# Bias rows of a highway gate, in 64-column pieces among the shifted value matmuls of windowed attention

## Chip, cores and metric

One core of one Trainium2 chip. The metric is the device time of one execution in microseconds (us); the median of the runs is compared.

## What is computed

Attention with a sliding window of 128 keys and 4 sink keys (batch 4, 8 heads, 768 positions, 64 columns a head), then a highway layer on the 3072 tokens of 512 columns:

```
scores = q @ k.T / 8
keep   = key < 4  or  0 <= query - key < 128
a      = softmax(where(keep, scores, -1e9))
x      = a @ v                                  # heads side by side: 3072 x 512
H      = max(x @ w_h, 0)
T      = 1 / (1 + exp(-(x @ w_t + b_t)))
out    = T * H + (1 - T) * x
```

## The kernel before

The tokens are cut into 24 blocks of 128 queries (`n` = 0 to 23, six to a batch element). Everything of one block is done by named steps, and the string `ORDER` writes out by hand, as `step:block`, in which order the steps are issued. Each engine works through its own share of that list strictly in order; semaphores connect the engines. The schedule is software-pipelined: the scores of block n+1 stand ahead of the value product of block n, and the highway products of block n-1 behind it.

The steps that matter here, with the line that a profile shows for each:

- `Tq`, `Tk` or the first part of `S` (PE, L318): transposes of q and k; `tq`, `tk`, `tt` copy them to SBUF (ScalarE, L323 and L330; a `V` in the name puts the copy on VectorE).
- `S` (PE): scores. L371 are the 64 x 128 parts, L384 the 64 x 64 corner parts, in all four 64 x 64 quadrants of the array.
- `x0_`, `x1_`, `xx` (ScalarE, L393, L398): exponentials into `e`; `m0_`, `m1_`, `mm` (VectorE, L404): masks on them.
- `sk`, `es` (PE L353, ScalarE L360): scores of the sink keys and their exponentials.
- `A` (PE): the value product. L429 are sixteen shifted matmuls in two of the four quadrants (keys of the neighbouring blocks), L448 eight full ones, L454 two for the sinks. `A` also issues the loads for the block eight ahead on GpSimd's queue.
- `xh` (VectorE, L462 and L467): divides by the row sum, giving x.
- `X` (PE, L481): transposes x into spare columns of the same accumulator `av`; `xT` (ScalarE, L486) or `xTV` (VectorE, L486) copies that to SBUF.
- `Mh`, `Mt` (PE, L509 and L497): the two highway products; `u` (ScalarE, L502): tanh for the gate.
- `d`, `U`, `e`, `o` (VectorE, L515, L521, L526, L531): the blend; `o` also issues the store on SP.
- `wA` (PE, L646): warm-up matmuls on an unused accumulator.
- `Ta`, `Ha`, `Tb`, `Hb`, `ua`, `da`, and so on: the last block's highway layer in two halves.

Two facts set the order around the change. There is one `av` accumulator (`bufs=1`), so `A` of block n must come after the `xT` copy of block n-1. And there are two PSUM banks `m0` and `m1` for all of `sk`, `Mh` and `Mt`; the string `M_BANKS` says which of the two each request gets, in order. A request waits until the last reader of that bank is done: `es` for `sk`, `d` for `Mh`, `u` for `Mt`.

The bias of the gate is added on PE: a matrix with ones in one row, times `bt16`, which holds half the bias in rows 0 and 64. For blocks 8 to 22 this is done ahead of time, at the start of `A` of the next block, by two matmuls of 64 rows, 64 output partitions and 512 columns in the two quadrants on the diagonal (`pe_bias`, L437). For blocks 0 to 7 it is one full matmul at the start of `Mt` (L494).

Of the kernel before, what the change touches and what calls it, by code (L numbers as in the profile page):

```python
# [8 lines left out]
FP16 = mybir.dt.float16  # L9
# [11 lines left out]
def kernel(  # L21
# [18 lines left out]
    nc = tc.nc  # L40
    P = 128

    B, H, S, D = q.shape
# [17 lines left out]
    const = ctx.enter_context(tc.tile_pool(name="const", bufs=1))  # L61
# [24 lines left out]

    ctx.callback(close_s)
    HP = P // 2
    B0 = 9
    M0 = 9  # L90
    NV = AHEAD + 5
    NS4 = H * NSINK
# [43 lines left out]
    bt32 = const.tile([P, DM], FP32, tag="bt32")  # L136
    bt16 = const.tile([P, DM], FP16, tag="bt16")
    ones_row = const.tile([P, P], FP16, tag="ones_row")
    ones2 = const.tile([P, P], FP16, tag="ones2")
    kf_first = const.tile([P, H, D], FP32, tag="kf0", name="kf0")  # L140
    ident32 = const.tile([P, P], FP32, tag="ident32")
    ident2 = const.tile([P, P], FP16, tag="ident2")
# [45 lines left out]
    with tc.manual_schedule(engines={ENG.Pool, ENG.SP}):  # L188
# [7 lines left out]
        for b in range(B):  # L196
            nc.sync.dma_start(out=vs_dn[b], in_=v[b, :, 0:NSINK, :])
        nc.gpsimd.affine_select(
            out=ident, in_=ident, compare_op=ALU.is_equal, fill=0.0,
# [14 lines left out]
            out=bm, in_=bm, compare_op=ALU.is_ge, fill=0.0,  # L214
            base=0, pattern=[[-NSINK, H]], channel_multiplier=1)
        nc.gpsimd.affine_select(
            out=bm, in_=bm, compare_op=ALU.is_ge, fill=0.0,
# [39 lines left out]
    def bias_rows(_):  # L257
        nc.vector.memset(bt16, 0.0)
        nc.vector.memset(ones_row, 0.0)
        nc.vector.memset(ones_row[0:1, :], 1.0)  # L260
        nc.vector.tensor_copy(out=ones2, in_=ones_row)
        nc.vector.memset(ones2[HP:HP + 1, :], 1.0)

    def bias_half(_):
        for r in (0, HP):
# [2 lines left out]
    def sink_ones(_):  # L268
# [3 lines left out]

    m_bank = [m_ps.tile([P, DM], FP32, tag=f"m{i}", name=f"m{i}") for i in range(2)]
    M_BANKS = (
        "010101010101010101010101010010100101001100101011010110101101"
    )
    m_next = iter(M_BANKS)

    def m_tile():
        return m_bank[int(next(m_next))]  # L280
# [7 lines left out]
    av_t, xh_of, xT_of, t_of, u_of, h_of, dd_of, ee_of, sk_of = {}, {}, {}, {}, {}, {}, {}, {}, {}  # L288
# [124 lines left out]
    def e_at(n, h):  # L413
        return e_of[n][:, h // 4, h % 2, (h // 2) % 2, :]

    def av_tile(n):
        if n not in av_of:
            av_of[n] = av_ps.tile([P, 2, 4, P], FP32, tag="av", name="av")
            av_t[n] = av_of[n]
        return av_of[n]  # L420

    def pe_AB(n):
        av = av_tile(n)
        nxt = v_ring[(n + 1) % NV]
        prv = v_ring[(n - 1 if n % NSC else n) % NV]
        lo, hi = slice(0, HP), slice(HP, P)
        for j in range(H):
            for src, part, vt, h in ((lo, hi, nxt, j), (hi, lo, prv, (j + 4) % H)):
                nc.tensor.matmul(  # L429
                    av[part, h // 4, h % 4, 0:_AVN], lhsT=e_at(n, h)[src, P:EW],  # L430
                    rhs=vt[src, 65 * h:65 * h + _AVN], start=(h % 4 == 0), stop=False,
                    skip_group_check=True)

    def pe_bias(n):
        t_of[n] = m_tile()
        for rows in (slice(0, HP), slice(HP, P)):
            nc.tensor.matmul(t_of[n][rows, :], lhsT=ones2[rows, rows], rhs=bt16[rows, :],  # L437
                             start=True, stop=False, skip_group_check=True)

    def pe_A(n):  # L440
        if n >= B0:
            pe_bias(n - 1)
        pe_AB(n)
        av = av_of[n]
        vt = v_ring[n % NV]
        b, c = divmod(n, NSC)
        for h in range(H):
            nc.tensor.matmul(  # L448
                av[:, h // 4, h % 4, 0:_AVN], lhsT=e_at(n, h)[:, 0:P],
                rhs=vt[:, 65 * h:65 * h + _AVN], start=False,  # L450
                stop=False, skip_group_check=True)
        if c:
            for g in range(2):
                nc.tensor.matmul(  # L454
                    av[:, g, :, 0:65], lhsT=es_of[n],
                    rhs=vs_bd[b % 2][:, 4 * g:4 * g + 4, :], start=False, stop=True,
                    skip_group_check=True)
        av_of[n] = av.rearrange("p g h e -> p (g h) e")
# [178 lines left out]
    def do_A(n):  # L637
        pe_A(n)
        load_set(n + AHEAD)
# [5 lines left out]
    def spare(t):  # L645
# [12 lines left out]
        "Mh": pe_Mh, "Mt": pe_Mt, "u": act_u, "U": dve_U, "d": dve_d, "e": dve_e, "o": dve_o,  # L658
        "mz0_": first_mask, "mz1_": second_mask, "id": identities, "ma": clear_ks,
        "na": clear_vs, "mc": bias_rows, "fa": lambda _: fill_ks(0, nc.vector), "fb": bias_half,  # L660
        "fc": sink_ones, "fd": lambda _: sink_v(0, nc.vector), "cv": convert_v,
        "wA": lambda n: spare(av_tile(n)[:, 0].rearrange("p a b -> p (a b)")),
# [8 lines left out]
    }  # L671
    ORDER = """
    mz0_:0 ma:0 na:0 Tq:0 na:1 Tk:0 tq:0 mz1_:0 tk:0 ma:1 wA:0 wA:0 Tk:1 mc:0 cv:0 tk:1 fa:0
    wA:0 wA:0 wA:0 S:0 cv:1 x0_:0 fb:0 x1_:0 wA:0 wA:0 wA:0 wA:0 Tq:3 m0_:0 fc:0 tq:3 wA:0 Tk:2
    tk:2 m1_:0 fd:0 wA:0 wA:0 wA:0 wA:0 Tq:1 A:0 tq:1 S:1 xh:0 sk:1 x0_:1 x1_:1 Tq:2 m0_:1 X:0
    sk:3 xTV:0 es:1 Tk:3 m1_:1 tq:2 tk:3 wA:1 A:1 es:3 S:2 xh:1 x0_:2 x1_:2 Tk:4 m0_:2 sk:2
    tkV:4 X:1 es:2 m1_:2 S:3 xT:1 A:2 x0_:3 Mh:1 x1_:3 xh:2 tq:4 d:1 X:2 tk:5 Mh:0 xTV:2 m0_:3
    Mh:2 d:0 m1_:3 S:4 d:2 Mt:0 x0_:4 x1_:4 m0_:4 A:3 u:0 m1_:4 Mt:1 tq:5 xh:3 tk:6 U:0 sk:4 u:1
    e:0 S:5 es:4 o:0 X:3 x0_:5 U:1 sk:5 xTV:3 e:1 A:4 x1_:5 m0_:5 o:1 tq:6 Mt:2 xh:4 tk:7 es:5
    u:2 m1_:5 X:4 S:6 xT:4 U:2 e:2 A:5 x0_:6 o:2 Mh:3 x1_:6 xh:5 tq:7 Mh:4 m0_:6 tk:8 m1_:6 X:5  # L680
    d:3 S:7 xT:5 d:4 A:6 x0_:7 Mh:5 xh:6 x1_:7 Mt:3 d:5 tq:8 tk:9 m0_:7 X:6 u:3 m1_:7 Mt:5 xT:6
    U:3 e:3 sk:7 o:3 u:5 Tq:9 es:7 U:5 Mt:4 tq:9 e:5 o:5 S:8 u:4 U:4 A:7 x0_:8 e:4 o:4 Mt:6
    x1_:8 xh:7 tq:10 Mh:6 m0_:8 tk:10 m1_:8 u:6 X:7 d:6 S:9 xT:7 U:6 A:8 e:6 xx:9 o:6 sk:9 xh:8
    Mh:7 es:9 tt:9 mm:9 Mt:7 d:7 X:8 u:7 S:10 xTV:8 U:7 A:9 e:7 xx:10 o:7 Mt:8 xh:9 tt:10 Mh:8
    mm:10 u:8 X:9 d:8 S:11 xT:9 U:8 A:10 e:8 xx:11 o:8 sk:11 xh:10 Mt:9 es:11 tt:11 mm:11 Mh:9
    u:9 X:10 d:9 S:12 xT:10 U:9 A:11 e:9 xx:12 o:9 Mt:10 xh:11 tt:12 Mh:10 mm:12 u:10 X:11 d:10
    S:13 xT:11 U:10 A:12 e:10 xx:13 o:10 sk:13 xh:12 Mt:11 es:13 tt:13 mm:13 Mh:11 u:11 X:12
    d:11 S:14 xT:12 U:11 A:13 e:11 xx:14 o:11 Mh:12 xh:13 tt:14 Mt:12 mm:14 X:13 d:12 u:12 S:15
    xT:13 U:12 e:12 xx:15 A:14 o:12 sk:15 xh:14 Mt:13 tt:15 mm:15 es:15 X:14 S:16 u:13 xTV:14
    U:13 A:15 xx:16 Mh:14 xh:15 tt:16 Mt:14 d:14 mm:16 Mh:13 u:14 U:14 sk:17 d:13 X:15 es:17  # L690
    S:17 xT:15 e:13 e:14 A:16 xx:17 o:13 o:14 Mt:15 xh:16 tt:17 Mh:15 mm:17 u:15 X:16 S:18 d:15
    xT:16 U:15 A:17 xx:18 e:15 o:15 Mh:16 xh:17 tt:18 Mt:16 mm:18 X:17 u:16 S:19 xTV:17 d:16
    A:18 xx:19 U:16 e:16 sk:19 xh:18 Mt:17 es:19 mm:19 tt:19 Mh:17 o:16 u:17 X:18 S:20 d:17
    xT:18 U:17 A:19 xx:20 e:17 o:17 Mh:18 xh:19 tt:20 Mt:18 mm:20 X:19 u:18 S:21 xTV:19 d:18
    A:20 xx:21 U:18 e:18 sk:21 o:18 Mt:19 es:21 xh:20 tt:21 Mh:19 mm:21 u:19 X:20 S:22 d:19
    xT:20 U:19 A:21 xx:22 e:19 o:19 Mh:20 xh:21 tk:24 Mt:20 mm:22 X:21 u:20 S:23 xTV:21 d:20
    A:22 xx:23 U:20 e:20 sk:23 xh:22 Mt:21 es:23 mm:23 X:22 u:21 Mh:21 xT:22 o:20 A:23 d:21 U:21
    Mt:22 xh:23 e:21 X:23 u:22 Mh:22 xTV:23 o:21 Ta:23 d:22 Ha:23 ua:23 U:22 e:22 Tb:23 da:23
    o:22 Hb:23 ub:23 db:23 ea:23 eb:23 pa:23 pb:23
    """  # L700

    with tc.manual_schedule(engines={ENG.PE, ENG.DVE, ENG.Activation, ENG.SP, ENG.Pool}):
        warm_up(8)
        identities(0)
        for step in ORDER.split():
            op, n = step.split(":")
# [36 lines left out]
```

## Time and profile before

| | us |
|---|---|
| Median of 3 runs | 122.24 |
| Lowest, highest | 121.48, 125.95 |
| The profiled execution: device time | 121.67 |
| The profiled execution: first to last instruction (span) | 119.5 |
| PE busy | 107.5 |
| VectorE (DVE) busy | 105.0 |
| ScalarE (ACT) busy | 87.8 |
| GpSimd (POOL) busy | 72.6 |
| Old bias pairs (L437), 30 matmuls | 5.9 |
| Full bias matmuls (L494), 8 matmuls | 3.0 |

Times within the profile count from its first instruction. PE matmuls are pipelined and overlap in the records: one 512-column matmul is shown with 0.38 us, while four in a row start 0.22 us apart. So starts are compared, not lengths. In the timeline a row gives the start, the length up to the end of the last instruction of the group, the engine, the line, the operation, the tiles and shapes, the number of instructions, and in brackets the idle time of the engine before it with what ended it.

### The profile page before, as it was taken

To read this page: it belongs to the slowest core of one execution; us is meant where nothing else is said; L and a number is where in the kernel's file an instruction comes from. 1 tells how busy PE (TensorE), PEld (TensorE's weight loads), DVE (VectorE), ACT (ScalarE), POOL (GpSimd) and SP (SyncE) were. 2 spreads that over 40 slices of the span, in tenths; PEclk is the share of its full clock that TensorE was granted. 3 is DMA by queue.
4 is the path that set the end of the run, shared out by engine and by line. 5 is a ranking of instruction groups with operands and counts; after the bars stand their busy time and mean duration, and the time that the engine had idled before them with its cause. 6 is when DMAs were issued, how large, how long until landed. Compare 5 with 4: busy or idle time off the path is not lost.

```text
span 119.5 us, 4971 instructions
## 1 busy us (share of the span) xinstructions
PE 107.5 (90%) x2119; PEld 65.5 (55%) x2119; DVE 105.0 (88%) x252; ACT 87.8 (73%) x123; POOL 72.6 (61%) x97
## 2 busy tenths in 40 slices
PE   5998676999899999799998999999999999999920
PEld 1443454655765546556754665657556665565610
DVE  6889666596999899999999999969999999999990
ACT  2248196929998978788898999987998979773210
POOL 5999886959799799967779999986000000000000
PEclk9999999999999999999999999999999999999995
DMA  2999999999999999999999999999920222011132
GB/s 55 217 172 153 146 180 174 194 153 151 128 194 209 207 137 183 191 205 205 177 195 219 118 198 157 205 203 157 207 84 12 89 92 93 26 67 73 52 139 88
DMA packets 79848, 17.64 MB, mean 148 GB/s; under 512 B 75602, under 2 KB 76882, under 8 KB 79828
## 3 DMA queue, kind: packets, MB, share of 16 engines
q0 software_dynamic: 71888, 9.97, 134.2%
q1 hardware_dynamic: 6884, 7.12, 19.2%
q10 hardware_dynamic: 1056, 0.26, 1.3%
q8 instruction: 16, 0.26, 0.9%
q14 instruction: 4, 0.03, 0.1%
HBM read 21.01 MB, written 6.29 MB: 228 GB/s over the span
## 4 chain that ended last, share of the span: by engine, by line
PE 63%; DVE 16%; DMA 7%; ACT 4%; issue 3%; POOL 3%; DVEq 0%; ACTq 0%
PE m L509 15%; PE m L497 11%; DMA qsd<-in_q_dram 7%; PE av L448 6%; PE av L429 6%; PE sps L384 4%; PE sps L318 4%; PE sps L371 4%; PE av L481 4%; DVE xh L467 4%; DVE otok L531 3%; PE av L454 3%; ACT e L393 3%; PE m L353 2%; DVE e L404 2%
## 5 line engine op out<-in xcount | busy, mean ns | idle before, releaser
L404 DVE TENSOR_TENSOR e<-e,mask 128x768 f16<-128x768 f16 (+1 forms) x33 | 24.8, 758 | 2.4 <-ACT e L393 2.3
L398 ACT ACTIVATE e<-sps,ebias 128x1536 f16<-128x1536 f32 x15 | 23.1, 1542 | 3.2 <-PE sps L384 3.0
L121 POOL DMA_DIRECT2D v<-in_v_dram x26 | 22.2, 854 | 4.7 <-DVE t L323 1.0
L509 PE MATMUL m<-wh_sb,xT 128*128 128x512 f16 x92 | 23.5, 379 | 0.3 <-issue 0.3
L497 PE MATMUL m<-wt_sb,xT 128*128 128x512 f16 x92 | 23.6, 379 | 0.0
L114 POOL DMA_DIRECT2D ksd<-in_k_dram x26 | 22.3, 861 | 2.0 <-DMA v<-in_v_dram 1.8
L107 POOL DMA_DIRECT2D qsd<-in_q_dram x23 | 21.2, 924 | 1.0 <-DMA qsd<-in_q_dram 0.5
L393 ACT ACTIVATE e<-sps,ebias 128x768 f16<-128x768 f32 x18 | 15.3, 898 | 5.3 <-PE sps L384 4.8
L502 ACT ACTIVATE u<-m 128x512 f16<-128x512 f32 x23 | 13.7, 597 | 6.5 <-PE m L497 6.3
L467 DVE TENSOR_TENSOR xh<-av,rec 128x512 f16<-128x512 f32 x24 | 16.6, 691 | 0.8
L531 DVE SCALAR_TENSOR_TENSOR otok<-xh,ee 128x512 f32<-128x512 f16 x23 | 15.8, 688 | 0.6
L515 DVE SCALAR_TENSOR_TENSOR dd<-m,xh 128x512 f16<-128x512 f32 x23 | 15.7, 686 | 0.1
L509 PEld LDWEIGHTS <-xT 128*128 128x128 f16 x92 | 8.6, 98 | 9.1 <-issue 1.0
L497 PEld LDWEIGHTS <-xT 128*128 128x128 f16 x92 | 8.8, 98 | 8.0
L330 ACT COPY tt<-sps 128x1024 f16<-128x1024 f16 x13 | 13.0, 999 | 0.0
L323 ACT COPY t<-sps 128x512 f16<-128x512 f16 x19 | 10.4, 590 | 2.1 <-PE sps L318 2.1
L429 PEld LDWEIGHTS <-e 64*64 64x64 f16 x384 | 9.9, 107 | 2.7 <-issue 1.9
L429 PE MATMUL av<-v,e 64*64 64x66 f16 x384 | 10.8, 193 | 0.4 <-DVE xT L486 0.3
L448 PE MATMUL av<-v,e 128*128 128x66 f16 x192 | 10.4, 195 | 0.0
L526 DVE TENSOR_TENSOR ee<-u,dd 128x512 f16<-128x512 f16 x23 | 9.7, 427 | 0.7
L486 ACT COPY xT<-av 128x512 f16<-128x512 f16 x15 | 8.7, 581 | 1.7 <-PE av L481 1.6
L481 PEld LDWEIGHTS <-xh 64*128 64x128 f16 x192 | 4.2, 95 | 10.2 <-DVE xh L467 7.4
(94 smaller groups left out, 173.5 us busy)
## 6 DMA issues: line engine op xcount, KB each, us to landing
out_dram<-otok SPq DMA_DIRECT2D x23, 256.0 KB, 4.7
qsd<-in_q_dram POOLq DMA_DIRECT2D x23, 128.0 KB, 7.2
ksd<-in_k_dram POOLq DMA_DIRECT2D x19, 128.0 KB, 7.1
v<-in_v_dram POOLq DMA_DIRECT2D x19, 128.0 KB, 7.1
wh_sb<-in_moe_w_h_dram POOLq DMA_DIRECT2D x1, 512.0 KB, 7.9
wt_sb<-in_moe_w_t_dram POOLq DMA_DIRECT2D x1, 512.0 KB, 8.4
ksd<-in_k_dram POOLq DMA_DIRECT2D x7, 64.0 KB, 6.9
v<-in_v_dram POOLq DMA_DIRECT2D x7, 64.0 KB, 6.3
```

The lines of the kernel that those rows point to most:

```text
L107: nc.gpsimd.dma_start(out=qsd, in_=q[b, :, c * P:(c + 1) * P, :].transpose([1, 0, 2]))
L114: nc.gpsimd.dma_start(out=ksd[rows], in_=k[b, :, s0:s0 + nr, :].transpose([1, 0, 2]))
L121: nc.gpsimd.dma_start(out=vt[rows, :, 0:D], in_=v[b, :, s0:s0 + nr, :].transpose([1, 0, 2]))
L393: nc.scalar.activation(out=e_tile(n)[:, g].rearrange("p a b c -> p a (b c)"), in_=s_tile(n, g)[:, :, 0:2 * EW], func=AF.Exp, bias=ebias, s ...
L398: nc.scalar.activation(out=e_tile(n).rearrange("p g a b c -> p (g a) (b c)"), in_=s_of[n][:, :, 0:2 * EW], func=AF.Exp, bias=ebias, scale= ...
L404: nc.vector.tensor_tensor(out=ev, in0=ev, in1=m.unsqueeze(1).to_broadcast([P, k, EW]), op=ALU.mult)
L429: nc.tensor.matmul(av[part, h // 4, h % 4, 0:_AVN], lhsT=e_at(n, h)[src, P:EW], rhs=vt[src, 65 * h:65 * h + _AVN], start=(h % 4 == 0), sto ...
L448: nc.tensor.matmul(av[:, h // 4, h % 4, 0:_AVN], lhsT=e_at(n, h)[:, 0:P], rhs=vt[:, 65 * h:65 * h + _AVN], start=False, stop=False, skip_g ...
L467: nc.vector.tensor_tensor(out=xh.rearrange("p (h d) -> p h d", d=D), in0=av_of.pop(n)[:, :, 0:D], in1=rec_of.pop(n).unsqueeze(2).to_broadc ...
L497: nc.tensor.matmul(t_of[n], lhsT=xT[:, kc, :], rhs=wt_sb[:, kc, :], start=False, stop=(kc == NOC - 1), skip_group_check=True)
L509: nc.tensor.matmul(hps, lhsT=xT[:, kc, :], rhs=wh_sb[:, kc, :], start=(kc == 0), stop=(kc == NOC - 1))
L531: nc.vector.scalar_tensor_tensor(out=otok, in0=xh_of.pop(n), scalar=2.0, in1=ee_of.pop(n), op0=ALU.mult, op1=ALU.add)
```

## The change

The bias of the gate is no longer two matmuls of 512 columns ahead of the shifted value matmuls. It is sixteen matmuls of 64 columns: after each pair of shifted matmuls in `pe_AB` come two pieces, one in each of the diagonal quadrants. A table `T_BESIDE` says which block's bias is hosted by which `A`. From block 9 on these are the same blocks as before; the bias of blocks 1, 2, 3, 6 and 7, which was a full matmul in `Mt`, is now hosted too, by `A` of blocks 3, 4, 6, 7 and 8. Blocks 0, 4 and 5 keep the full matmul. `ones_row` now has its ones in two half rows, so that it serves both forms, and `ones2` is dropped.

`M_BANKS` and `ORDER` are written anew for it. PE's own order of steps is the same but for one `wA` more. On ScalarE and VectorE some steps change place or engine: `tq:3` and `xT:4` go to VectorE; `xT:19`, `xT:21` and `xT:23` go to ScalarE; `xTV:3` stands ahead of `U:1`; `o:1`, `o:2`, `e:16` and `o:20` are moved; `es:21` stands behind `tt:21`; at the end `e:21` stands ahead of `xh:23`.

```diff
-    B0 = 9
+    T_BESIDE = {3: 1, 4: 2, 6: 3, 7: 6, 8: 7, 9: 8, 10: 9, 11: 10, 12: 11, 13: 12, 14: 13, 15: 14, 16: 15, 17: 16, 18: 17, 19: 18, 20: 19, 21: 20, 22: 21, 23: 22}
...
-        nc.vector.memset(ones_row[0:1, :], 1.0)
-        nc.vector.tensor_copy(out=ones2, in_=ones_row)
-        nc.vector.memset(ones2[HP:HP + 1, :], 1.0)
+        nc.vector.memset(ones_row[0:1, 0:HP], 1.0)
+        nc.vector.memset(ones_row[HP:HP + 1, HP:P], 1.0)
...
-        "010101010101010101010101010010100101001100101011010110101101"
+        "010101010101010010101000101101011010110011010100101001010010"
...
+        m = T_BESIDE.get(n)
+        if m is not None:
+            t_of[m] = m_tile()
         for j in range(H):
             for src, part, vt, h in ((lo, hi, nxt, j), (hi, lo, prv, (j + 4) % H)):
                 nc.tensor.matmul(
                     av[part, h // 4, h % 4, 0:_AVN], lhsT=e_at(n, h)[src, P:EW],
                     rhs=vt[src, 65 * h:65 * h + _AVN], start=(h % 4 == 0), stop=False,
                     skip_group_check=True)
-
-    def pe_bias(n):
-        t_of[n] = m_tile()
-        for rows in (slice(0, HP), slice(HP, P)):
-            nc.tensor.matmul(t_of[n][rows, :], lhsT=ones2[rows, rows], rhs=bt16[rows, :],
-                             start=True, stop=False, skip_group_check=True)
+            if m is not None:
+                cols = slice(D * j, D * j + D)
+                for part in (lo, hi):
+                    nc.tensor.matmul(
+                        t_of[m][part, cols], lhsT=ones_row[part, part], rhs=bt16[part, cols],
+                        start=(j == 0), stop=False, skip_group_check=True)
 
     def pe_A(n):
-        if n >= B0:
-            pe_bias(n - 1)
         pe_AB(n)
...
-    A:18 xx:19 U:16 e:16 sk:19 xh:18 Mt:17 es:19 mm:19 tt:19 Mh:17 o:16 u:17 X:18 S:20 d:17
-    xT:18 U:17 A:19 xx:20 e:17 o:17 Mh:18 xh:19 tt:20 Mt:18 mm:20 X:19 u:18 S:21 xTV:19 d:18
-    A:20 xx:21 U:18 e:18 sk:21 o:18 Mt:19 es:21 xh:20 tt:21 Mh:19 mm:21 u:19 X:20 S:22 d:19
-    xT:20 U:19 A:21 xx:22 e:19 o:19 Mh:20 xh:21 tk:24 Mt:20 mm:22 X:21 u:20 S:23 xTV:21 d:20
-    A:22 xx:23 U:20 e:20 sk:23 xh:22 Mt:21 es:23 mm:23 X:22 u:21 Mh:21 xT:22 o:20 A:23 d:21 U:21
-    Mt:22 xh:23 e:21 X:23 u:22 Mh:22 xTV:23 o:21 Ta:23 d:22 Ha:23 ua:23 U:22 e:22 Tb:23 da:23
-    o:22 Hb:23 ub:23 db:23 ea:23 eb:23 pa:23 pb:23
...
+    d:16 A:18 xx:19 U:16 sk:19 xh:18 Mt:17 es:19 mm:19 tt:19 Mh:17 e:16 u:17 X:18 o:16 S:20
+    xT:18 d:17 A:19 xx:20 U:17 e:17 Mh:18 o:17 tt:20 xh:19 Mt:18 mm:20 X:19 u:18 S:21 xT:19 d:18
+    xx:21 A:20 U:18 e:18 o:18 sk:21 Mt:19 tt:21 xh:20 es:21 mm:21 u:19 Mh:19 U:19 X:20 d:19 S:22
+    xT:20 e:19 xx:22 A:21 o:19 Mh:20 xh:21 tk:24 Mt:20 mm:22 X:21 d:20 u:20 S:23 xT:21 U:20 e:20
+    xx:23 A:22 o:20 sk:23 xh:22 Mt:21 es:23 mm:23 X:22 u:21 Mh:21 xT:22 U:21 A:23 d:21 e:21
+    Mt:22 xh:23 o:21 u:22 X:23 Mh:22 xT:23 U:22 Ta:23 d:22 Ha:23 ua:23 e:22 Tb:23 da:23 o:22
+    Hb:23 ub:23 ea:23 db:23 eb:23 pa:23 pb:23
```

## The prediction

> **What bounds the kernel now.** I read the page first (busy shares, then the chain that ended last), then stretches of 8 us by engine, then the timeline around the calls that the change touches.
>
> ```profile
> PE 107.5 (90%) x2119; PEld 65.5 (55%) x2119; DVE 105.0 (88%) x252; ACT 87.8 (73%) x123; POOL 72.6 (61%) x97
> PE 63%; DVE 16%; DMA 7%; ACT 4%; issue 3%; POOL 3%; DVEq 0%; ACTq 0%
> ...
> 30.00:54.00 24.00, 22.80 (x479) 14.17 (x478) 22.90 (x46) 20.65 (x34) 21.77 (x27) 1.00 2.28 182
> 54.00:62.00 8.00, 8.00 (x189) 5.06 (x180) 7.79 (x16) 7.21 (x10) 5.85 (x9) 1.00 2.17 194
> ```
>
> The columns after the length are busy time of PE, PEld, DVE, ACT and POOL. Two engines are full at once. From 30 to 54 us the chain runs mostly through DVE; from 54 to 110 us mostly through PE, a block every 3.7 us (4.1 with a sink step), with DVE at 97%.
>
> The decisive view is what ends PE's wait before A of a block. Block 11, then 14:
>
> ```profile
> 61.30 0.29 PE L481 MATMUL av<-ident,xh 64*128 64x64 f16 x8
> 61.63 0.59 ACT L486 COPY xT<-av 128x512 f16<-128x512 f16 x1
> 61.98 0.32 PE L384 MATMUL sps<-tt 64*64 64x64 f16 x16
> 62.12 0.39 PE L437 MATMUL m<-bt,ones 64*64 64x512 f16 x2
> 62.27 0.45 PE L429 MATMUL av<-v,e 64*64 64x66 f16 x16
> ...
> 73.28 0.60 ACT L502 ACTIVATE u<-m 128x512 f16<-128x512 f32 x1 [0.28 <-PE m L497]
> 73.78 0.58 ACT L486 COPY xT<-av 128x512 f16<-128x512 f16 x1
> 73.94 0.39 PE L437 MATMUL m<-bt,ones 64*64 64x512 f16 x2
> 74.41 0.45 PE L429 MATMUL av<-v,e 64*64 64x66 f16 x16
> ```
>
> xT:n-1 reads the one av buffer that A:n overwrites. It ends at 61.63+0.59 = 62.22 and the shifted value matmuls (L429) start at 62.27; in block 14 at 74.36 and 74.41. In all fifteen blocks with a bias pair L429 starts 0.05 to 0.07 us behind the end of that copy. PE issues its last score matmul at about 61.98+0.32-0.20 = 62.10, so the pair at 62.12 only fills a wait of 0.17 us. The chain names L437 because the pair runs there, not because it decides.
>
> **What the skill says.** "TensorEngine Tiling (Array Packing)", Key Properties: tiles work independently, and a change of tiling mode drains the array. The trace agrees: L384 uses all four 64x64 quadrants, and its 16 matmuls start within 0.32-0.20 = 0.12 us, 0.03 us for each four; L429 uses two quadrants, and its 8 pairs start within 0.45-0.19 = 0.26 us, also 0.03 us a pair. The same page, Gotcha 1, warns of two row tiles in one PSUM bank; the old pair already writes one bank from both row halves, to different partitions. "PSUM — Partial Sum Buffer", The four PSUM rules: a starting matmul clears the written-bits of its whole bank in the quadrants that it writes, and a later one without start overwrites where the bit is clear. So start on piece 0 alone does what the change needs; no time follows from it.
>
> ```profile
> 108.89 0.40 PE L437 MATMUL m<-bt,ones 64*64 64x512 f16 x2
> 108.96 0.45 PE L429 MATMUL av<-v,e 64*64 64x66 f16 x16
> 109.34 0.33 PE L448 MATMUL av<-v,e 128*128 128x66 f16 x5
> ...
> 21.67 0.44 PE L429 MATMUL av<-v,e 64*64 64x66 f16 x16
> 22.05 0.43 PE L448 MATMUL av<-v,e 128*128 128x66 f16 x8
> ```
>
> Block 23 has the pair 0.07 us ahead of L429, so both run together; block 2 has none. L429 to L448 is 0.38 us in both: bias beside the shifted matmuls is already free.
>
> **The change part by part.**
>
> *1. The fifteen old pairs go (blocks 9 to 23).* Gain 0: the wait for xT stays and is now bare.
>
> *2. Sixteen pieces in each of 20 calls of A.* PE gets 20x16 = 320 matmuls and loses 30+5, and one warm-up is added. Not shown before: eight groups of four in a row, with a reload of the ones each time. Below: 0 (a gain is excluded, since xT sets the start). Above: the pieces take turns with the shifted pairs, 8x0.032 = 0.26 us a call. I take 0 by the L384 row, which has the same four quadrants and as many loads. The first piece is a new wait inside A: for the last reader of its bank. Behind it on PE stand the rest of A and all that follows. From block 9 that reader is u:n-2, as for the old pair, and it ends ahead of xT. For the early hosts it is d:2 (ends 26.79, A:3 starts 27.79), es:4 (30.78 against 31.83), d:3 (about 37.5 against 38.3), es:7 (43.98 against 45.57) and u:6 (48.88 against 50.12): cost 0.
>
> *3. Five full bias matmuls go (Mt of 1, 2, 3, 6, 7).* L494 to L497 is 0.22 us (52.31 to 52.52), together 1.1 us of PE. At 28 to 50 us DVE is the queue that is late, so I book nothing directly; Mt:7's counts in 5.
>
> *4. DVE from 28 to 50 us.* xTV:3 ahead of U:1 and the copy of xT:4 moved from ACT to DVE let A:4 start about 0.2 us and A:5 about 0.5 us earlier, but DVE gains one copy of 0.42 us. Its queue from the end of o:0 (31.16) to the end of d:4 (39.25) was full but for 0.13 us: 39.25+0.41-0.13 = 39.53. Mh:5 now takes the bank of d:4 (before, of d:3) and so starts at 39.58 instead of 39.43; Mh:5 takes 0.86+0.17 us to its end, d:5 waits for it, 40.66 instead of 40.49: **+0.17 us**, which the full DVE queue carries on to 54 us. POOL work here also stretches DVE (two L404 took 1.86 us at 41.10 against 0.55 each at rest, beside L181 on POOL): the shift may move that by ±0.8 us.
>
> *5. The new bank string.* Holding t7 from A:8 leaves one bank for sk:9 and Mh:7, so Mh:7 waits for es:9.
>
> ```profile
> 51.44 1.03 PE L509 MATMUL m<-wh_sb,xT 128*128 128x512 f16 x4
> 51.71 0.45 ACT L360 ACTIVATE es<-m,ebias 32x256 f16<-32x256 f32 x1
> ...
> 54.24 0.42 DVE L486 COPY xT<-av 128x512 f16<-128x512 f16 x1
> 54.71 0.45 PE L429 MATMUL av<-v,e 64*64 64x66 f16 x16
> ```
>
> Mh:7 moves from 51.44 to 51.71+0.45+0.05 = 52.21; minus the 0.22 us of Mt:7's bias, X:8 comes near 53.97 instead of 53.48. xTV:8 sits behind mm:9 and d:7 on DVE and ran at 54.24; with +0.17 on DVE it runs at 54.41, and X:8 is done by 54.26. A:9 starts 0.17 us late. From A:9 to A:19 queue orders on PE and ACT are unchanged: the offset stays, **sum so far +0.17**.
>
> *6. xT:19 and xT:21 go from DVE to ACT.*
>
> ```profile
> 97.04 0.60 ACT L502 ACTIVATE u<-m 128x512 f16<-128x512 f32 x1 [0.27 <-PE m L497]
> 97.40 0.42 DVE L486 COPY xT<-av 128x512 f16<-128x512 f16 x1
> 97.87 0.45 PE L429 MATMUL av<-v,e 64*64 64x66 f16 x16
> ...
> 99.43 0.45 ACT L360 ACTIVATE es<-m,ebias 32x256 f16<-32x256 f32 x1
> 100.06 1.03 PE L509 MATMUL m<-wh_sb,xT 128*128 128x512 f16 x4
> ```
>
> On ACT the copy queues behind u:18, as block 14 shows (u at 73.28, copy 0.50 us later). So 97.04+0.50+0.58+0.05 = 98.17 for A:20 against 97.87: **+0.29**. Then es:21 now stands behind tt:21. xx:21 begins at 98.0 as before, tt:21 at 99.45, es:21 0.89 us later at 100.34, ending at 100.79. Mh:19 has the bank of es:21: 100.84, where 100.06+0.29 = 100.35 was due: **+0.49**, less 0.1 us by which PE came late to X:20 before (101.02, where Mh:19's four would have let it start at 100.06+0.86 = 100.92). A:21 comes near 102.66 against 101.99 (+0.67). In block 22 u:20 began at 104.85: 104.85+0.67+0.50+0.58+0.05 = 106.65 against 105.61: **+1.04** in all for this part. A:23 is bound by xT:22 and keeps it. DVE, 0.42 us lighter in each of the two blocks, is no help: PE is what runs late there.
>
> *7. The tail.* xTV:23 (0.42 us at 111.36) leaves DVE, and e:21 stands ahead of xh:23. Da waits for PE's L569, so of 0.42 us about 0.41 is kept: **-0.42**. The rest (tq:3 on DVE and one copy of ones fewer before 13 us, one more warm-up, fb, fc) lies in front of A:0, which starts at 13.6 after a DMA wait with the mask 0.7 us ready: 0. The steps o:1, o:2, e:16 and o:20 are moved by under 2 us; each o also issues its block's store on SP, which has nothing else queued, and otok has four buffers: 0. The loads that each A issues on POOL keep their order; the ones of A:4 and A:5 go out a little earlier.
>
> Sum: +0.17+1.04-0.42 = **+0.8 us**. Against the profiled execution's 121.67 us (span 119.5 and 2.2 around it): 122.5. The median of the three runs is 122.24, the lowest 121.48; the profile lies in the lower half, so I say 122.7.
>
> **The rivals.**
> *A, slower: the pieces are not hidden.* Place: the L429 run of A:9 to A:23. Price: up to 0.26 us x 15 = 3.8, with the five early hosts behind DVE: 122.5+3.8 = 126.3. It decides once a group of four takes more than about 0.05 us instead of 0.03. For it: 64 instructions in 0.26 us is a longer burst than L384's, and three banks are written at once. Against: the L384 and block 23 rows. Chance 0.24.
> *B, a little faster: the stalls of 5 and 6 don't appear* because the queues shift by themselves, and the early starts of A:4 and A:5 are kept: 121.67-0.42-0.4 = 120.9. For it: A:5 really has 0.5 us; against: DVE has one copy more. Chance 0.13.
> *C, clearly faster: the pair was real PE time*, 0.14 us from L437 to L429: 15x0.14+5x0.22 = 3.2, 118.5. Against: L429 sits at the end of xT in fifteen of fifteen. Chance 0.07.
> The forecast has 0.56.
>
> **How the numbers follow.** The forecast's own range is 121.5 to 123.9: ±0.8 for POOL beside DVE, and PE issue gaps (0.31 and 0.79 us were seen at 64.6 and 18.95) with 13% more PE instructions. To hold 8 in 10 it reaches down to B and up to A: 120.9 to 126.3. Within 2% (119.8 to 124.7, about what a measurement of this kernel can tell from no change): B, the forecast but 0.05, and some of A. Faster by over 2% is C; slower is A and that 0.05.
>
> **What would show it.** Right: starts of L429's successor still 0.05 us behind an xT copy in every hosted block; first shifted matmul to L448's first still 0.38 us; A:20 and A:22 0.3 to 0.5 us further behind their score matmuls; Mh:7 and Mh:19 behind es; PE busy lower in 28 to 50 us without an earlier A:9. Wrong: 0.5 us or more in place of 0.38 (A); A starting right behind the scores (C); A:9 before 54.3 (B).

## The result, and the profile after

The changed kernel takes 130.7 us in the median (130.1 to 133.4) against 122.7: ratio 1.065, 95% interval 1.054 to 1.077. The forecast was 122.7 with a range up to 126.3. It is slower, and by far more than the steps of the sum or the slower rival allowed.

Executions of one kernel scatter by some per cent, the longer ones often at a lower mean clock of the array: the ratios leave the longer ones out, and since the profiled execution (133.37 us, span 131.7) is one of them, places and kinds of loss are read from it and amounts from the comparisons. From its page, the busy line, the clock row in 40 slices, the instruction queue and the chain by engine:

```profile
PE 110.9 (84%) x2405; PEld 67.2 (51%) x2405; DVE 104.3 (79%) x250; ACT 88.4 (67%) x124; POOL 72.2 (55%) x97
...
PEclk9999999999999999998569999559999999999997
...
q8 instruction: 19, 0.31, 0.9%
...
PE 48%; DVE 22%; issue 12%; ACT 6%; DMA 5%; POOL 3%; DVEq 0%; ACTq 0%
```

"issue", time in which the engine waited for nothing that the profile shows, went from 3% to 12% of the chain. DVE has no more work than before. The clock has two dents that were not there. The waits of PE on "issue" (total us, times, longest), both of the kernel before and then the four longest after:

```profile
PE sps L384 <- issue: 0.8, 1, 0.8
PE m L509 <- issue: 0.3, 1, 0.3
...
PE m L437 <- issue: 4.0, 2, 2.5
PE av L447 <- issue: 2.9, 1, 2.9
PE m L508 <- issue: 0.7, 1, 0.7
PE m L351 <- issue: 0.7, 1, 0.7
```

In the timeline the long ones after are single holes, in the midst of matmuls that wait for no one:

```profile
55.58 0.19 PE L437 MATMUL m<-bt,ones_row 64*64 64x64 f16 x1 [1.55 <-issue]
...
62.55 0.60 PE L447 MATMUL av<-v,e 128*128 128x66 f16 x8 [2.88 <-issue]
...
83.06 0.26 PE L437 MATMUL m<-bt,ones_row 64*64 64x64 f16 x1 [2.50 <-issue]
```

The key is where they stand. Count PE's records (weight loads, matmuls and its few semaphore instructions) in order of start. Every one of these holes stands at number 194 plus a multiple of 256: 962, 1218, 1986, 2242 and 3010 in this profile. In the kernel before, the two holes, 0.8 us at 19.7 us and 0.3 us at 64.9 us, stand at 450 and 2242: the same series. Call these numbers borders. And q8 is, by its counts, the queue of PE's own instructions: 16 packets for 4279 records before, 19 for 4852 now, one packet of 16 KB for each border. Its line before:

```profile
q8 instruction: 16, 0.26, 0.9%
```

So PE runs out of instructions. The trace has the start of each q8 packet. While the loads of q, k and v run (to 85 us) it begins 1.1 to 4.6 us after PE has passed the border before (3.0 in the mean), takes 0.9 to 1.5 us, and at every long hole PE resumes 1.3 to 1.8 us after it has landed. When the loads have ended the packets begin 0.6 us after the border in the mean (from 0.9 us ahead of it to 1.8 behind), and no hole is left. In the kernel before the packets are no earlier: 2.9 us behind the border in the mean while the loads run. What has changed is how soon PE needs them. The hole at 62.55: border passed at 55.58, packet from 60.11 to 61.07, resumed at 62.55.

In this execution the holes have a second price. The window of the hole, and that of the work behind it (busy PE, PEld, DVE, ACT, POOL, then the granted clock):

```profile
59.60:62.55 2.95, 0.07 (x9) 0.09 (x1) 0.94 (x2) 1.24 (x1) 1.98 (x4) 0.82 2.23 185
62.55:67.36 4.81, 4.81 (x22) 2.19 (x22) 1.76 (x3) 1.85 (x3) 4.69 (x7) 0.50 1.92 167
```

After 2.9 us without work the clock is 0.50 through the 4.8 us that follow. The same steps (A of block 10 from L447 on, sk, Mt, Mh) took 2.5 us in the kernel before: 2.3 us more, and by the same reckoning about as much again after 83.06. Holes (7.2 us more than before) and dents (4.6) together come to 11.8 of the 12.2 us by which this profile is longer. The other executions bear less of it: the one with a mean clock of 0.996 took 130.1 us, those with 0.973 and 0.974 took 129.7 to 130.8, so most of the loss is there without a dent.

The Trainium skill, "TensorE: Matmul & The Clock Gate", Part 1, has the array's clock halved after an idle window of some 3.4 us. Here shorter holes did it, though not always: in all the profiles, seven of the eight holes of over 2 us (2.1 to 3.0 from start to start) were followed by a dent of 3.4 or 6.8 us, and one of 2.7 us, in the changed kernel shifted by 112 records, was not.

What the forecast did see is there too:

```profile
117.62 0.22 PE L430 MATMUL av<-v,e 64*64 64x66 f16 x2 [0.53 <-ACT xT L485]
...
118.00 0.43 PE L447 MATMUL av<-v,e 128*128 128x66 f16 x8
```

From the first shifted matmul to the first full one it is 0.38 us, with sixteen pieces between as without; it is 0.36 to 0.38 us in 16 of the 20 hosted blocks; of the others, three have a hole between the two and one lies in a dent. And A waits for xT.

### The profile page after: what moved, and what is told of

It is laid out like the page before. It is cut to its first block, busy times and chain, and to the rows that moved or that the text cites. A ratio compares the mean times of both kernels' runs of the same rounds, so it can differ in the third digit from the quotient of the medians.

```text
span 131.7 us, 5545 instructions
## 1 busy us (share of the span) xinstructions
PE 110.9 (84%) x2405; PEld 67.2 (51%) x2405; DVE 104.3 (79%) x250; ACT 88.4 (67%) x124; POOL 72.2 (55%) x97
## 3 DMA queue, kind: packets, MB, share of 16 engines
q0 software_dynamic: 71888, 9.97, 124.4%
## 4 chain that ended last, share of the span: by engine, by line
PE 48%; DVE 22%; issue 12%; ACT 6%; DMA 5%; POOL 3%; DVEq 0%; ACTq 0%
PE m L508 11%; PE m L496 9%; DMA qsd<-in_q_dram 5%; PE av L447 5%; DVE xh L466 5%; DVE otok L530 5%; PE av L430 3%; PE sps L316 3%; DVE dd L514 3%; DVE e L402 3%; PE av L480 3%; PE sps L369 3%; PE m L351 3%; PE av L453 3%; PE sps L382 3%
## 5 line engine op out<-in xcount | busy, mean ns | idle before, releaser
L508 PE MATMUL m<-wh_sb,xT 128*128 128x512 f16 x92 | 24.4, 390 | 1.6 <-ACT es L358 0.9
L402 DVE TENSOR_TENSOR e<-e,mask 128x768 f16<-128x768 f16 (+1 forms) x33 | 23.8, 731 | 2.2 <-ACT e L391 2.2
L496 PE MATMUL m<-wt_sb,xT 128*128 128x512 f16 x92 | 25.4, 401 | 0.0
L530 DVE SCALAR_TENSOR_TENSOR otok<-xh,ee 128x512 f32<-128x512 f16 x23 | 16.5, 720 | 0.6
L461 DVE RECIPROCAL rec<-av 128x8 f32<-128x8 f32 x24 | 4.9, 203 | 13.3 <-PE av L453 12.2
L508 PEld LDWEIGHTS <-xT 128*128 128x128 f16 x92 | 8.8, 100 | 11.3 <-issue 3.8
L496 PEld LDWEIGHTS <-xT 128*128 128x128 f16 x92 | 9.2, 103 | 8.3 <-issue 1.1
L447 PE MATMUL av<-v,e 128*128 128x66 f16 x192 | 10.8, 199 | 2.9 <-issue 2.9
L437 PE MATMUL m<-bt,ones_row 64*64 64x64 f16 x320 | 9.4, 198 | 4.0 <-issue 4.0
L430 PE MATMUL av<-v,e 64*64 64x66 f16 x384 | 11.3, 196 | 1.5 <-ACT xT L485 1.1
L430 PEld LDWEIGHTS <-e 64*64 64x64 f16 x384 | 9.9, 110 | 5.1 <-issue 4.2
L485 ACT COPY xT<-av 128x512 f16<-128x512 f16 x17 | 9.9, 581 | 3.9 <-PE av L480 3.8
L321 ACT COPY t<-sps 128x512 f16<-128x512 f16 x18 | 9.8, 591 | 2.0 <-PE sps L316 1.9
```

Source lines behind the costliest of these rows:

```text
L402: nc.vector.tensor_tensor(out=ev, in0=ev, in1=m.unsqueeze(1).to_broadcast([P, k, EW]), op=ALU.mult)
L430: nc.tensor.matmul(av[part, h // 4, h % 4, 0:_AVN], lhsT=e_at(n, h)[src, P:EW], rhs=vt[src, 65 * h:65 * h + _AVN], start=(h % 4 == 0), sto ...
L447: nc.tensor.matmul(av[:, h // 4, h % 4, 0:_AVN], lhsT=e_at(n, h)[:, 0:P], rhs=vt[:, 65 * h:65 * h + _AVN], start=False, stop=False, skip_g ...
L496: nc.tensor.matmul(t_of[n], lhsT=xT[:, kc, :], rhs=wt_sb[:, kc, :], start=False, stop=(kc == NOC - 1), skip_group_check=True)
L508: nc.tensor.matmul(hps, lhsT=xT[:, kc, :], rhs=wh_sb[:, kc, :], start=(kc == 0), stop=(kc == NOC - 1))
L530: nc.vector.scalar_tensor_tensor(out=otok, in0=xh_of.pop(n), scalar=2.0, in1=ee_of.pop(n), op0=ALU.mult, op1=ALU.add)
```

## The experiments

Three theories. R: PE's instruction stream is refilled in blocks of 256 records, and with the pieces PE outruns the refill while the loads hold up its packets. O: the new order and bank string cost the time. H: the pieces are not hidden in the array (rival A of the prediction). A median is given with the ratio to the kernel before in the same comparison where there is one.

**Pieces on the old order.** The kernel before, with only the pieces.

```diff
+        m = n - 1 if n >= B0 else None
...
+            if m is not None:
+                cols = slice(D * j, D * j + D)
+                for part in (lo, hi):
+                    nc.tensor.matmul(
+                        t_of[m][part, cols], lhsT=ones2[part, part], rhs=bt16[part, cols],
+                        start=(j == 0), stop=False, skip_group_check=True)
...
-        if n >= B0:
-            pe_bias(n - 1)
```

> The kernel before, its own order of steps and bank string, with only the bias of blocks 8 to 22 cut into sixteen pieces inside A of 9 to 23. PE has 2119-30+240 = 2329 matmuls and as many weight loads. Theory R (PE's instruction stream is refilled in blocks of 256 records and PE outruns the refill while the loads of q, k and v fill the DMA queues): 125 to 131 us, with PE gaps of 1 us and more that start at record 194 or at 194 plus a multiple of 256, and first shifted matmul to first full one still 0.38 us where no such gap lies between. Theory O (the new order and bank string cost the time): 121.5 to 123.5 us, as before. Theory H (the pieces are not hidden in the array): about 126 us, spread evenly, with 0.5 us or more in place of 0.38.

127.3 us, ratio 1.042 (1.035 to 1.050). The holes are at 2242, 2498 and 3010:

```profile
64.35 0.22 PE L439 MATMUL m<-bt,ones 64*64 64x64 f16 x2 [1.59 <-issue]
...
82.20 0.32 PE L384 MATMUL sps<-tt 64*64 64x64 f16 x16 [2.57 <-issue]
```

The second stands in the scores, where nothing was changed. In 14 of the 15 blocks with pieces it is 0.38 us from the first shifted matmul to the first full one, and the fifteenth has a hole between them: H, which asked for 0.5 us or more, does not show. O as the only cause falls.

**One piece on the new order.**

```diff
-            if m is not None:
-                cols = slice(D * j, D * j + D)
+            if m is not None and j % 8 == 0:
+                cols = slice(D * j, D * j + 8 * D)
```

> The changed kernel, its order, bank string and hosts, with the bias of each hosted block in one piece of 512 columns a quadrant (behind the first shifted pair) instead of eight of 64. PE has 2405-320+40 = 2125 matmuls. Theory R: 121.5 to 124.5 us, what the order alone costs is what is left (my steps gave +0.8). Theory O: 129 to 131 us. Theory H: 122 to 124 us, so it tells R and H from O only.

124.0 us, ratio 1.013 (1.004 to 1.022): the order, with its hosts and bank string, costs some 1.5 us, and the cutting into pieces the other 6.7 (130.7-124.0). One hole of over 0.5 us is left in its profile, 1.1 us at 63.5 us, on record 2242.

**Four pieces, and two.** The same edit with `j % 2` and 128 columns, and with `j % 4` and 256.

> The changed kernel with four pieces of 128 columns a quadrant instead of eight of 64: 2405-160 = 2245 matmuls. Theory R: between one piece and eight, 124 to 128 us, and not smooth, since it depends on which refill is late. Theory O: 129 to 131 us. Theory H (turns taken by column count): as with eight, 129 to 131 us.

> The changed kernel with two pieces of 256 columns a quadrant: 2405-240 = 2165 matmuls, between one piece (2125, 124.0 us) and four (2245, 127.8 us). Theory R: 124.5 to 126.5 us. If only long bursts of short matmuls hurt: 124.0, as with one piece.

Four: 127.8 us (124.5 to 129.5; too uneven for a ratio). Two: 124.4 us, ratio 1.014 (0.999 to 1.028). Two cost no more than one, as far as these runs can tell, though R had put them at 124.5 to 126.5. Four lie anywhere between two and eight. That would fit something that is overrun from about 2245 matmuls on, but the scatter of four is too wide to show a step. H had expected four to cost what eight cost, 129 to 131 us; three of the four executions are below that.

**The pair cut up at its own place**, ahead of the shifted matmuls, on the old order.

```diff
-            nc.tensor.matmul(t_of[n][rows, :], lhsT=ones2[rows, rows], rhs=bt16[rows, :],
-                             start=True, stop=False, skip_group_check=True)
...
+        for j in range(H):
+            cols = slice(D * j, D * j + D)
+            for rows in (slice(0, HP), slice(HP, P)):
+                nc.tensor.matmul(t_of[n][rows, cols], lhsT=ones2[rows, rows], rhs=bt16[rows, cols],
+                                 start=(j == 0), stop=False, skip_group_check=True)
```

> The kernel before with its old bias pair cut into sixteen matmuls of 64 columns at the pair's own place, ahead of the shifted value matmuls: 2119-30+240 = 2329 matmuls, as with the pieces between the shifted matmuls on the old order (127.3 us). Theory R (refill of PE's instructions, by their number): 125.5 to 129 us, with long gaps only at record 194 plus multiples of 256. Theory H (the trouble is in mixing the pieces with the shifted matmuls): 121.5 to 124 us.

126.9 us, ratio 1.036 (1.028 to 1.045), the same as between the shifted matmuls. The holes, one of them here, are at 450, 1986, 2242 and 3010. So it is the number of PE instructions, not where they stand. Nor do the pieces themselves hold up A: they start within 0.25 us, in the time in which A waits for xT anyway, and in the blocks without a hole the shifted matmuls stand 0.05 us behind xT in nine and 0.12 to 0.21 us in three. H falls.

```profile
64.01 0.32 PE L441 MATMUL m<-bt,ones 64*64 64x64 f16 x5 [2.27 <-issue]
```

**The stream shifted by 112 records.** The changed kernel, then the kernel before.

```diff
-        for _ in range(n):
-            nc.tensor.matmul(w, lhsT=warm[:, 0:P], rhs=warm, start=True, stop=True)
+        for i in range(8 * n):
+            c = slice(D * (i % 8), D * (i % 8) + D)
+            nc.tensor.matmul(w[:, c], lhsT=warm[:, 0:P], rhs=warm[:, c], start=True, stop=True)
```

> The changed kernel with the eight warm-up matmuls of 512 columns replaced by 64 of 64 columns, ahead of all work: 56 matmuls and 56 weight loads more, so every later step stands 112 records further on in PE's stream, at about the same time. Theory R: the long gaps stay at record 194 plus multiples of 256 and so fall some 112 records earlier in the work than before; the time stays within 128 to 132.5 us. If the gaps belonged to a place in the work (a bank, a wait), they would move to 112 records behind those borders.

> The kernel before with the same shift of 112 records by short warm-up matmuls. Theory R: PE's rate between the borders is what it was, just inside what the refill can follow, so the time stays within 121 to 124 us; the two gaps of 0.8 and 0.3 us move with the borders, and a better or worse place could give up to 1 us either way.

The changed kernel stays at 131.2 us (1.065, 1.055 to 1.076). Its long holes are at 706, 1218, 1474, 2242, 2498, 2754 and 3266 of the longer stream: the same series, 112 records earlier in the work. They belong to the count and to no step.

```profile
67.72 0.22 PE L438 MATMUL m<-bt,ones_row 64*64 64x64 f16 x2 [2.50 <-issue]
```

The kernel before, shifted, took 124.6 to 128.2 us in its three timed runs, where I had expected 121 to 124; its profile was taken in an execution in which the array ran at a clock of 0.57 from start to end, so it can't show why. Whether this kernel is only just inside what the refill can follow, so that the place of the borders matters, stays open. That execution does show one thing: with PE near half speed, a block of 256 records lasts 5.6 us and more, and no border has a hole.

**Fewer loads.** No loads of v from chunk 13 on (a chunk is the 128 keys of a block), so the value products of those blocks read older chunks; in the changed kernel, and as a control in the kernel before.

```diff
-            load_v(n + 1)
+            if n + 1 <= NV - 1:
+                load_v(n + 1)
```

> The changed kernel, with the loads of v for chunks 13 to 24 left out (the value products of those blocks read what older chunks left), so GpSimd issues about a third less load traffic from A:4 on. PE's instructions are the same 2405 matmuls. Theory R: the refill waits less behind load packets; the gaps at the 256-record borders shrink to under 1 us each and the time falls to 123 to 127 us. Theories O and H: no change beyond 1 us, 129 to 131 us.

> The control of the run with fewer loads: the kernel before without the loads of v for chunks 13 to 24. Theory R: the kernel before lost only about 1.4 us in the two gaps at 19.7 and 64.9 us, so 120.5 to 122.5 us. If fewer loads help for another reason than the refill (a shorter wait for data, GpSimd less in VectorE's way), the gain would be as large as in the changed kernel, 4 to 5 us: 117 to 119 us.

Changed: 126.0 us, ratio 1.032 (1.026 to 1.039), where all loads gave 1.065. Control: 121.2 us, 0.990 (0.981 to 0.998). Fewer loads are worth 3% to the changed kernel and 1% to the other. The holes of the changed kernel shrink from 8.6 us in all to 4.4, but not each to under 1 us, as I had expected: the longest is 1.6. Nor do the packets come much sooner while there are loads, 2.8 us behind the border in the mean. What differs is that the last load packet ends at 74.5 us instead of 85.5, and no hole stands behind that. Together with the packets of the other profiles, 2.8 to 3.3 us late during the loads in every kernel at full clock and 0.4 to 1.6 us behind them, this says that the refill comes late while loads run; no run took all the loads away.

**Longer runs in the loads.** The loads from block 8 on read 2 KB in one piece a partition instead of eight times 256 B, which gives those blocks other values.

```diff
+            fq, fk, fv = (t.rearrange("b h s d -> (b h s d)").rearrange("(r h d) -> r h d", h=H, d=D)[c]
+                          for t in (q, k, v))
...
+            nc.gpsimd.dma_start(out=qsd, in_=fq)
```

> The changed kernel, in which the loads of q, k and v from block 8 on read contiguous 2 KB runs instead of eight runs of 256 B a partition (the same bytes to the same tiles, but other values than the blocks need). PE's instructions are unchanged. Theory R with the delay set by the number of load packets ahead of the refill: the gaps at the 256-record borders all but go, 121 to 124 us. Theory R with the delay set by bytes: 126 to 130 us. Theory O: 129 to 131 us.

128.6 us, ratio 1.039 (1.026 to 1.053), within what was expected if bytes set the delay. The load queue has 44176 packets instead of 71888, yet the q8 packets begin 3.0 us after their border while the loads run, as before. So the number of packets alone is not what holds them up. Bytes, or the time in which the 16 DMA engines are taken (the DMA row of the page still shows 9 tenths), would fit; which of them is open, and so is why this kernel is still faster than the changed one.

**The new order, taken apart.** On the kernel before: the last copy alone on ScalarE, and then step 6 alone.

```diff
-    Mt:22 xh:23 e:21 X:23 u:22 Mh:22 xTV:23 o:21
+    Mt:22 xh:23 e:21 X:23 u:22 Mh:22 xT:23 o:21
```

> The kernel before with one step moved as in the change: the copy of the last block's xT goes from VectorE to ScalarE (xTV:23 to xT:23). My step 7 by itself: -0.4 us, 122.3 against 122.7. If refills alone decide, PE's instructions are the same and nothing changes beyond 0.2 us. It is also the only piece of the change that I expect to gain anything, so a version that may beat both kernels.

```diff
-    ... X:19 u:18 S:21 xTV:19 d:18 A:20 xx:21 ... sk:21 o:18 Mt:19 es:21 xh:20 tt:21 Mh:19 ... S:23 xTV:21
+    ... X:19 u:18 S:21 xT:19 d:18 A:20 xx:21 ... sk:21 o:18 Mt:19 tt:21 xh:20 es:21 Mh:19 ... S:23 xT:21
```

> The kernel before with my step 6 alone: the copies xT:19 and xT:21 go from VectorE to ScalarE and es:21 stands behind tt:21 (there is one bank string and one bias pair a block as before). By my sums +1.0 us in blocks 20 to 22, 123.7 against 122.7: A:20 0.3 us and A:22 0.4 us further behind their score matmuls, and a wait of Mh:19 or Mh:20 for es:21. If the order costs nothing: 122.7 within 0.3.

The tail: ratio 1.001 (0.997 to 1.006), no gain. Step 6: 124.3 us, ratio 1.013 (1.005 to 1.020), as much as the whole new order with one piece. No version that computes the same beat the kernel before.

All kernels in one table; the ratio is to the kernel before in the same comparison, and the last column sums the holes of over 0.45 us at a border in the profiled execution, each less the 0.13 us that a step there takes at most:

```
kernel                        PE matmuls  median us  ratio  profiled span  holes
before                              2119      122.7  1              119.5    1.4
before, last copy on ScalarE        2119      123.4  1.001          121.2    2.0
before, step 6 alone                2119      124.3  1.013          124.1    1.3
before, fewer v loads               2119      121.2  0.990          121.6    2.8
one piece, new order                2125      124.0  1.013          121.0    1.6
two pieces, new order               2165      124.4  1.014          122.6    1.9
before, shifted by 112 *            2175      127.6  -              162.8    0.0
four pieces, new order              2245      127.8  -              124.8    5.5
pieces, old order                   2329      127.3  1.042          125.5    4.7
pair cut up in place, old order     2329      126.9  1.036          126.7    6.2
changed (eight pieces)              2405      130.7  1.065          131.7    8.6
changed, fewer v loads              2405      126.0  1.032          123.8    4.4
changed, long runs                  2405      128.6  1.039          127.8    8.3
changed, shifted by 112             2461      131.2  1.065          128.2    8.0
* profiled at a clock of 0.57
```

The holes follow the times roughly, not exactly. Some are in the kernel before as well, and their sum changes from one profile of the same PE stream to the next (1.3 to 2.8 us at 2119 matmuls).

## Why the prediction was wrong

*Step 2 failed.* It asked whether sixteen more matmuls fit into the array and took 0. That was right: 0.38 us in the blocks without a hole. It did not ask whether they can be fed. The page had the means: 2119 matmuls with as many loads, 16 instruction packets, two "issue" gaps inside a row of matmuls. An estimate from the trace: in a block of 3.9 us PE had about 176 records, so 256 of them lasted some 5.7 us; with 28 more they last 4.9 us. Border to packet, packet, and 1.5 us to resume come to 3.0+1.0+1.5 = 5.5 us in the mean, up to 7.1. By this estimate the kernel before stood just at that line, and the change crossed it. The forecast named the 0.31 and 0.79 us gaps and the 13% more instructions, but took them as a part of its spread of 1.2 us either way and put no cost on the instructions themselves. Price: 6.7 us, by the runs with eight pieces and with one.

The Trainium skill, *"Runtime: NRT & Kernel Launch", Instruction fetch mechanics,* states the blocks of 256 instructions and that the sequencer (the part of an engine that issues its instructions) fetches the next one by its own DMA queue; the trace agrees on both, with borders 256 records apart and one q8 packet for each. It also calls the cost of a border "mostly hidden"; here it was up to 2.9 us, and the measurement decides.

*Step 1 held.* L430 stands 0.05 us behind xT in 13 of the 20 hosted blocks, and taking the pair away freed nothing.

*Steps 3 and 4 held in part.* From A:0 to A:5 it is 21.1 us against 21.5 before (forecast 0.5 us earlier); from A:0 to A:9 41.0 against 41.1, where I had forecast 0.17 us more, and that with 1.4 us of holes in between (0.8 before). The holes of this stretch, where VectorE is late, cost nothing that can be seen.

*Step 5's wait appeared,* but did not decide A:9, which came right behind its scores (xT was done 0.07 us before, and the last score matmul had started 0.02 us before):

```profile
50.67 0.45 ACT L358 ACTIVATE es<-m,ebias 32x256 f16<-32x256 f32 x1
51.17 1.02 PE L508 MATMUL m<-wh_sb,xT 128*128 128x512 f16 x4 [0.60 <-ACT es L358]
...
53.33 0.42 DVE L485 COPY xT<-av 128x512 f16<-128x512 f16 x1
...
53.82 0.20 PE L430 MATMUL av<-v,e 64*64 64x66 f16 x2
```

*Step 6 held,* in kind and in size: the copy queues behind u, which began at 107.90, and Mh:19 waits for es:21. A:20 starts 0.47 us behind its last score matmul instead of 0.19, A:22 0.72 instead of 0.35. From A:18 to A:22, a stretch without a hole, it is 16.47 us against 15.33: 1.14 us more, where the sum had 1.04. In the run with step 6 alone the cost was 1.3% (0.6 to 2.5 us).

```profile
108.39 0.58 ACT L485 COPY xT<-av 128x512 f16<-128x512 f16 x1
...
111.19 0.46 ACT L358 ACTIVATE es<-m,ebias 32x256 f16<-32x256 f32 x1
...
111.71 0.59 PE L508 MATMUL m<-wh_sb,xT 128*128 128x512 f16 x2 [0.33 <-ACT es L358]
```

*Step 7 failed.* It let da wait for PE's L569 (now L568). The chain's tail, in the profile with only that copy moved, shows da (L582) 0.02 us behind the end of ua:

```profile
114.42 0.45 PE sps L569 x4
...
114.96 0.39 ACT u L574
115.35 0.02 issue
115.37 0.04 DVE dd L582
```

In the kernel before it was the same, ua ending at 113.74 and da at 113.78. ua stood between, so VectorE had slack and the copy was hidden. So nothing of the forecast 0.42 us was gained. The row was on the chain that I read; I took the engine in front of ua for the releaser.

*The rivals.* A was right in sign and wrong in mechanism: it priced turns in the array, which the 0.38 us and the pair cut up in place exclude. B had two of its parts right, the early A:5 and a wait of step 5 that cost A:9 nothing; A:9 even stands before its mark of 54.3 us, at 53.82, but in this execution A:0 had itself begun 0.8 us earlier. B too priced no refill. C was excluded by the same view as forecast: L430 still waits for xT.

## What to carry to other kernels

Before cutting one matmul into many on an engine that is nearly full, count its instructions per microsecond, not only its columns: here, by the estimate above, 256 records had to last about 5.5 us while loads were running, and a kernel near that line paid 6.7 us for work that the array did for nothing. Holes in a row of matmuls that wait for nothing are worth numbering: if they stand a fixed number of records apart, look at the instruction queue before looking at the code around them. Where two forms cost the array the same, as one piece and eight did here, the one with fewer and longer matmuls is the safer.

## What the runs showed of the hardware that was not expected

- Refill holes of up to 2.9 us on PE, only at borders 256 records apart, with the q8 packet starting 1.1 to 4.6 us behind the border while loads ran and 0.6 us in the mean when they had ended; PE resumed 1.2 to 2.0 us after the landing at every hole of over 0.45 us in these runs.
- Seven of eight holes of over 2 us were followed by a stretch of 3.4 or 6.8 us at half the granted clock. In the profile of the changed kernel such a stretch cost about 2.3 us, nearly as much again as its hole.
- Four 64 x 64 quadrants took 32 matmuls and their 32 weight loads in the 0.38 us that 16 and 16 take, with no loss, as long as the instructions were there.
